# Attention and two MLPs on one core: the first product of each MLP by seven Strassen products, its result kept in DRAM, the second product summed in PSUM

## The chip, the cores and the metric

One core of a Trainium2 chip runs the whole program. The metric is device time in microseconds; three runs of the kernel before lie between 1133.15 and 1134.03 us. The engines are named as in the profile: PE (matmuls) with PEld (its weight loads), DVE (VectorE), ACT (ScalarE), POOL (GpSimd), SP (the DMA queue that issues nearly all transfers).

## The reference

Sigmoid attention over 4 batches, 12 heads, 448 tokens and 64 columns per head, then two MLPs on the 1792 x 768 result, each 768 -> 2048 -> 768. All weights arrive as 64-bit floats; everything else is 32-bit.

```python
scores = scale * np.matmul(q, k.transpose(0, 1, 3, 2)) - np.log(S)
attn = 1.0 / (1.0 + np.exp(-scores))
x = np.matmul(attn, v)                       # then (B*S, H*D) = (1792, 768)
h = x @ w_in                                 # layer 0, w_in 768 x 2048
g = np.where(h > 0.0, h, np.exp(np.minimum(h, 0.0)) - 1.0)
x = g @ w_out
h = x @ w_in                                 # layer 1
g = h - np.tanh(h)
out = g @ w_out
```

## The kernel before, in words

Each operand of a matmul is split into a head (rounded to the matmul's type) and a rest, and every product of 128x128 weights is three matmuls: head by head, head by rest, rest by head. A split is one ACT copy (head) and one DVE subtraction (rest).

**Order.** `Sched` takes operations with a queue, an estimated cost, what they come after and a rank, simulates the five queues and emits in the order that this gives. On a chip each engine runs its queue in that order. Attention's operations are chained per queue by the due times of `PHASES`; those of the MLP come in by their rank.

**Attention.** 24 pairs of heads. Per pair: transposes of q and k, scores (L344), sigmoid (L355), its split `ah` (L364 to L370), `pv` (L382) into one PSUM tile, the values' split on POOL (L329, L334). `xhead` (ACT, L389) and `xrest` (DVE, L394) put the result, split, into X; the next pair's first `pv` waits for `xrest`.

**MLP.** Per layer 8 groups of two hidden chunks of 128 (`GC`, `NG`). For each group and each of four token blocks (512, 384, 384, 512 wide: `AT`) `m_h` (L547) makes each chunk's 18 matmuls: 6 slices of the 768 inputs, three matmuls each. `g_a`, `g_b`, `g_c` (L553 to L573) apply the nonlinearity, `g_head` and `g_rest` (L580, L584) split it, `m_o` (L588 to L615) makes the group's share of the second product, and `p_add` (L617 to L623) adds it to the sum P in SBUF; the first group is a copy by ACT (L621). So first and second products alternate. At layer 0's end `x_head` and `x_rest` (L626, L629) split P into X; at layer 1's end `store` writes P to `out`.

**Weights.** Each chunk of 128x768 64-bit values is loaded (L486) into one of two buffers, `first` and `second`, narrowed to 32 bits by one ACT and three DVE operations (L496 to L511) and split (L524, L528). The load of a chunk waits for the split of the chunk two before it.

## Time and profile before

| | |
|---|---|
| runs, median (range) | 1133.44 us (1133.15 to 1134.03), 3 runs |
| profiled execution, first to last instruction | 1131.9 us, 1.5 us under the median |
| PE / PEld busy | 1122.2 / 1025.5 us |
| DVE / ACT / POOL busy | 727.7 / 476.4 / 61.6 us |
| granted PE clock | 1.00 throughout |
| attention's last `pv` ends | 204.9 us |
| DMA moved | 73.3 MB, mean 65 GB/s |

The chain of waits goes back from the last instruction to what released it, so its shares say what the time was spent on in a row; a group row has an operation's busy time, the mean of one in ns, and the idle time of its engine just before. Durations reported for neighbouring operations overlap by some 0.07 us on DVE.

### The profile page before, as it was taken

To read this page: it belongs to the slowest core of one execution; us is meant where nothing else is said; L and a number is where in the kernel's file an instruction comes from. 1 tells how busy PE (TensorE), PEld (TensorE's weight loads), DVE (VectorE), ACT (ScalarE), POOL (GpSimd) and SP (SyncE) were. 2 spreads that over 40 slices of the span, in tenths; PEclk is the share of its full clock that TensorE was granted. 3 is DMA by queue.
4 is the path that set the end of the run, shared out by engine and by line. 5 is a ranking of instruction groups with operands and counts; after the bars stand their busy time and mean duration, and the time that the engine had idled before them with its cause. 6 is when DMAs were issued, how large, how long until landed. Compare 5 with 4: busy or idle time off the path is not lost.

```text
span 1131.9 us, 14882 instructions
## 1 busy us (share of the span) xinstructions
PE 1122.2 (99%) x6020; PEld 1025.5 (91%) x6020; DVE 727.7 (64%) x1117; ACT 476.4 (42%) x743; POOL 61.6 (5%) x112
## 2 busy tenths in 40 slices
PE   8999999999999999999999999999999999999998
PEld 7888888998989898989898989999999999999897
DVE  6888889735575757575757793557474847575644
ACT  6777778654333333333334554523131313131310
POOL 4323223000000000000000000000000000000000
PEclk9999999999999999999999999999999999999999
DMA  6334332211111111111202020303020202121124
GB/s 157 89 82 98 84 81 84 85 56 56 56 56 56 56 56 57 54 58 38 75 29 84 28 84 22 91 4 96 14 86 27 84 28 84 29 84 28 56 66 130
DMA packets 86900, 73.31 MB, mean 65 GB/s; under 512 B 50096, under 2 KB 81072, under 8 KB 86832
## 3 DMA queue, kind: packets, MB, share of 16 engines
q1 hardware_dynamic: 85312, 71.85, 21.8%
q8 instruction: 47, 0.77, 0.3%
q10 hardware_dynamic: 1520, 0.52, 0.2%
q14 instruction: 21, 0.17, 0.0%
HBM read 66.85 MB, written 5.51 MB: 64 GB/s over the span
## 4 chain that ended last, share of the span: by engine, by line
PE 98%; SPq 0%; DMA 0%; POOL 0%; DVE 0%; ACT 0%; issue 0%; ACTq 0%
PE hps L547 41%; PE ops L610 21%; PE ops L597 20%; PE pvps L382 9%; PE sps L344 5%; PE tps L302 2%; DMA first<-in_q_dram 0%; SPq L233 0%; ACT a L355 0%; DVE ah L370 0%; POOL vs L329 0%; SPq L214 0%; POOL vs L334 0%; DVE ah L366 0%; SPq L237 0%
## 5 line engine op out<-in xcount | busy, mean ns | idle before, releaser
L623 DVE TENSOR_TENSOR P<-P,ops 128x384 f32<-128x384 f32 (+1 forms) x364 | 209.4, 580 | 62.0 <-PE ops L610 33.9
L547 PE MATMUL hps<-X,e 128*128 128x512 f32 (+1 forms) x1152 | 242.2, 363 | 0.0
L547 PE MATMUL hps<-X,wi 128*128 128x512 f32 (+1 forms) x1152 | 240.7, 362 | 0.0
L610 PE MATMUL ops<-wo,g 128*128 128x384 f32 x1344 | 238.3, 334 | 0.0
L597 PE MATMUL ops<-g,wo 128*128 128x512 f32 (+1 forms) x1152 | 235.8, 362 | 0.0
L610 PEld LDWEIGHTS ops<-wo,g 128*128 128x128 f32 x1344 | 234.0, 188 | 1.2
L597 PEld LDWEIGHTS ops<-g,wo 128*128 128x128 f32 x1152 | 208.4, 188 | 22.8
L547 PEld LDWEIGHTS hps<-X,e 128*128 128x128 f32 x1152 | 208.6, 188 | 22.5
L547 PEld LDWEIGHTS hps<-X,wi 128*128 128x128 f32 x1152 | 208.4, 188 | 22.7 <-DVE r L571 0.2
L382 PE MATMUL pvps<-ah,vs 128*128 128x448 f32 x504 | 122.8, 377 | 1.1 <-POOL vs L334 1.1
L580 ACT ACTIVATE g<-r 128x512 fp32r<-128x512 f32 (+1 forms) x128 | 73.9, 577 | 83.5 <-DVE r L573 48.0
L584 DVE TENSOR_TENSOR g<-r,g 128x512 fp32r<-128x512 f32 (+1 forms) x128 | 79.7, 622 | 44.9 <-ACT g L580 43.8
L382 PEld LDWEIGHTS pvps<-ah,vs 128*128 128x128 f32 x504 | 89.7, 188 | 13.7 <-issue 6.8
L560 ACT ACTIVATE r<-hps 128x512 f32<-128x512 f32 (+1 forms) x64 | 34.7, 542 | 144.8 <-PE hps L547 144.8
L370 DVE TENSOR_TENSOR ah<-a,ah 128x896 fp32r<-128x896 f32 x96 | 92.9, 988 | 3.2
L573 DVE TENSOR_TENSOR r<-hps,r 128x512 f32<-128x512 f32 (+1 forms) x64 | 39.8, 621 | 83.9 <-ACT r L560 83.8
L355 ACT ACTIVATE a<-sps,bias 128x896 f32<-128x896 f32 x96 | 85.1, 916 | 3.6 <-DVE ah L370 2.5
L571 DVE SCALAR_TENSOR_TENSOR r<-r,hps 128x512 f32<-128x512 f32 (+1 forms) x64 | 39.5, 617 | 66.8 <-ACT r L564 65.0
L558 ACT ACTIVATE r<-hps 128x512 f32<-128x512 f32 (+1 forms) x64 | 34.6, 541 | 109.8 <-PE hps L547 109.6
L344 PE MATMUL sps<-e 64*128 64x448 f32 (+1 forms) x504 | 69.2, 373 | 0.4 <-ACT a L355 0.4
L528 DVE TENSOR_TENSOR e<-first,e 128x768 fp32r<-128x768 f32 x16 | 15.3, 957 | 77.8 <-ACT e L524 77.8
L344 PEld LDWEIGHTS sps<-e 64*128 64x128 f32 (+1 forms) x504 | 52.7, 185 | 11.0 <-issue 6.3
(61 smaller groups left out, 685.4 us busy)
## 6 DMA issues: line engine op xcount, KB each, us to landing
first<-in_moe_w_in_dram SPq DMA_DIRECT2D x16, 768.0 KB, 4.7
second<-in_moe_w_in_dram SPq DMA_DIRECT2D x16, 768.0 KB, 4.6
first<-in_moe_w_out_dram SPq DMA_DIRECT2D x16, 768.0 KB, 4.4
second<-in_moe_w_out_dram SPq DMA_DIRECT2D x16, 768.0 KB, 4.2
kq<-in_q_dram SPq DMA_DIRECT2D x24, 112.0 KB, 2.7
first<-in_q_dram SPq DMA_DIRECT2D x22, 112.0 KB, 2.4
kq<-in_k_dram SPq DMA_DIRECT2D x18, 128.0 KB, 2.6
vl<-in_v_dram SPq DMA_DIRECT2D x12, 192.0 KB, 2.7
```

The source lines that it names most:

```text
L344: nc.tensor.matmul(out=ps[:, j, :S], lhsT=e[lanes, ks, cols], rhs=e[lanes, qs, :S], start=(x == 0), stop=(x == 2),)
L355: nc.scalar.activation(out=a[:, :m], in_=T.pop(("s", n, u))[:, :m, :S], func=ACTF.Sigmoid, bias=bias, scale=scale)
L370: nc.vector.tensor_tensor(out=t[:, 1, :m], in0=T.pop(("a", n, u))[:, :m], in1=f(t[:, 0, :m]), op=ALU.subtract)
L382: nc.tensor.matmul(out=ps, lhsT=vs[n % 2][:, vz, c:c + 128], rhs=t[:, az, j], start=(u == 0 and j == 0 and vz == 0 and az == 0), stop=(u = ...
L547: nc.tensor.matmul(out=ps, lhsT=wi[wz][:, kk], rhs=X[:, xz, kk, tokens(b)], start=(n == 0), stop=(n == 3 * KD - 1),)
L571: nc.vector.scalar_tensor_tensor(out=r, in0=r, scalar=-1.0, in1=h, op0=ALU.add, op1=ALU.max)
L573: nc.vector.tensor_tensor(out=r, in0=h, in1=r, op=ALU.subtract)
L580: nc.scalar.activation(out=gt[:, 0, c, half(b)], in_=T["g", i, g, b, c], func=ACTF.Copy)
L584: nc.vector.tensor_tensor(out=gt[:, 1, c, half(b)], in0=T.pop(("g", i, g, b, c)), in1=f(gt[:, 0, c, half(b)]), op=ALU.subtract)
L597: nc.tensor.matmul(out=ps, lhsT=wo[c][wz][:, e], rhs=gt[:, gz, c, half(b)], start=(n == 0), stop=(n == last),)
L610: nc.tensor.matmul(out=ps, lhsT=gt[:, gz, c, t0:t0 + 128], rhs=wo[c][wz].rearrange("p k f -> p (k f)")[:, e * DH:(e + 1) * DH], start=(n = ...
L623: nc.vector.tensor_tensor(out=acc, in0=acc, in1=ps, op=ALU.add)
```

## The change

Attention writes its result unsplit (`xdone` instead of `xhead` and `xrest`) into four tiles R0a, R0b, R1a, R1b: token half (1024 and 768 tokens) by half of the 768 columns. The MLP of a layer is two phases.

**Phase 1** has 8 groups of two hidden chunks by two token halves, called steps. With the two chunks, the two halves of the 768 inputs and the two halves of a step's tokens (512 or 384 each) as a 2x2 by 2x2 block product, `m_p` makes seven products of 9 matmuls (3 slices, three matmuls each) where eight would do it directly. Seven operands of each token half (B11, B21, B22 and the sums T1 to T4) are made once per layer; the weight side's sums S1 to S4 are made per group by POOL. Products that share a term share a PSUM bank: the bank is copied out (`snap`, ACT) and then summed onto by the next product, and `h_add` (DVE) joins it with the third. The nonlinearity follows, and `g_store` writes the hidden values unsplit to DRAM.

**Phase 2** goes over token blocks (512, 512, 384, 384 in layer 0; four of 384 and one of 256 in layer 1). For each of the 16 chunks it loads the hidden values back, splits them, and sums all 16 in PSUM over 48 matmuls per output tile; one copy takes the tile out. All of `w_out` lies split in SBUF, in the places of phase 1's operands. Twelve (layer 0) and 13 (layer 1) chunks of `w_out`, the 16 of layer 1's `w_in` and 2 of layer 0's are narrowed ahead and kept in DRAM as 32-bit values (`keep`); four chunks are narrowed during attention.

PE's order after attention is one written chain; in it each step's P4 stands behind the next step's P1. Other MLP operations are ranked by how late they may start. Core of the diff:

```diff
-            def xhead(n):
+            def xdone(n):
                 b, hp = pairs[n]
...
+                ps = T.pop(("o", n))
+                for z in range(2):
+                    lo, hi = max(b * S, T0[z]), min((b + 1) * S, T0[z] + 2 * HW[z])
+                    if lo < hi:
+                        t = raws[f"R{z}" + "ab"[hp // KH], 0].rearrange("p (k t) -> p k t", k=KH)
+                        nc.scalar.activation(
+                            out=t[:, hp % KH, lo - T0[z]:hi - T0[z]], in_=ps[:, lo - b * S:hi - b * S], func=ACTF.Copy
+                        )
...
+                if place == "W2":
+                    return ("R0a", 3 * CW, 4 * CW), ("R0b", 3 * CW, 4 * CW)
...
+            def w_sum(step, which, j0, j1):
...
+                out, x, y, op = {
+                    "S1": (s1, a21, a22, ALU.add), "S2": (s2, s1, a11, ALU.subtract),
+                    "S4": (s4, a12, s2, ALU.subtract), "S3": (s3, a11, a21, ALU.subtract),
+                }[which]
+                nc.gpsimd.tensor_tensor(out=out, in0=x, in1=y, op=op)
...
+            SUMS = {"T1": ("12", "12", "11"), "T2": ("12", "22", "12"), "T3": ("11", "12", "11"), "T4": ("21", "21", "12")}
...
+            def sums_on(i, s, x):
+                return "POOL" if (i, s) == (0, 1) and x != "T1" else "DVE"
...
+            PROD = {
+                "P1": ("B11", "W0", 0, "a", True), "P2": ("B21", "W0", 1, "b", True),
+                "P5": ("T1", "W1", 0, "d", True), "P6": ("T2", "W1", 1, "a", False),
+                "P3": ("B22", "W2", 1, "d", False), "P7": ("T3", "W2", 0, "a", False),
+                "P4": ("T4", "W3", 0, "a", False),
+            }
...
+            def m_p(step, p):
...
                 n = 0
-                for kk in range(KD):
+                for kk in range(KH):
                     for wz, xz in ((0, 0), (0, 1), (1, 0)):
+                        k0 = (half * KH + kk) * 128
                         nc.tensor.matmul(
-                            out=ps, lhsT=wi[wz][:, kk], rhs=X[:, xz, kk, tokens(b)],
-                            start=(n == 0), stop=(n == 3 * KD - 1),
+                            out=ps, lhsT=w[wz][:, k0:k0 + 128], rhs=xs[xz][:, kk],
+                            start=(opens and n == 0), stop=(n == 3 * KH - 1), skip_group_check=True,
                         )
                         n += 1
...
+            SNAP = {"s1": "a", "s2": "a", "s5": "d"}
+            ADD = {(0, 0): ("s1", "b"), (0, 1): ("s2", "d"), (1, 1): ("s5", "a")}
+
+            def snap(step, x):
+                s = step[2]
+                T["s", step, x] = t = temp(slot_of["s", step, x])[:, :HW[s]]
+                nc.scalar.activation(out=t, in_=T["ps", step, SNAP[x]], func=ACTF.Copy)
+
+            def h_add(step, c, b):
+                x, tag = ADD[c, b]
+                t = T["s", step, x]
+                nc.vector.tensor_tensor(out=t, in0=t, in1=T["ps", step, tag], op=ALU.add)
...
+                nc.sync.dma_start(
+                    out=hidden[i, n][:, t0:t0 + HW[s]], in_=T.pop(("s", step, "o" if (c, b) == (1, 0) else ADD[c, b][0]))
+                )
...
+            def g_load(i, k, n):
+                t0, w = blocks(i)[k]
+                T["graw", i, k, n] = t = temp(slot_of["graw", i, k, n])[:, :w]
+                nc.sync.dma_start(out=t, in_=hidden[i, n][:, t0:t0 + w])
...
+            PRODS = ("P1", "P2", "P5", "P6", "P3", "P7")
...
+                    ps = [("h", step, p) for p in PRODS]
+                    if n:
+                        ps.insert(1, ("h", mine_steps[n - 1], "P4"))
+                    sequence += ps
...
+                after = {
+                    "P6": [("snap", step, "s1")], "P3": [("snap", step, "s5")],
+                    "P7": [("snap", step, "s2")], "P4": [("h_add", step, 1, 1)],
+                }
...
+            sch.chain([("pv", last, 3)] + sequence)
```

## Rows read from the trace of the kernel before

**Rows 1.** The page, part 1: busy us of each engine (share of the span).

```profile
PE 1122.2 (99%) x6020; PEld 1025.5 (91%) x6020; DVE 727.7 (64%) x1117; ACT 476.4 (42%) x743; POOL 61.6 (5%) x112
```

**Rows 2.** The page, part 4: the chain that ended last, by engine, by line.

```profile
PE 98%; SPq 0%; DMA 0%; POOL 0%; DVE 0%; ACT 0%; issue 0%; ACTq 0%
PE hps L547 41%; PE ops L610 21%; PE ops L597 20%; PE pvps L382 9%; PE sps L344 5%; PE tps L302 2%; DMA first<-in_q_dram 0%; SPq L233 0%; ACT a L355 0%; DVE ah L370 0%; POOL vs L329 0%; SPq L214 0%; POOL vs L334 0%; DVE ah L366 0%; SPq L237 0%
```

**Rows 3.** Windows: busy us of each engine (instructions), PEclk, DMA share, GB/s.

```profile
0.00:15.00 15.00, 10.71 (x73) 9.05 (x73) 5.25 (x8) 6.84 (x10) 10.21 (x24) 1.00 0.72 168
...
250.00:650.00 400.00, 400.00 (x1992) 359.83 (x1991) 250.54 (x389) 150.74 (x241) 0.00 (x0) 1.00 0.17 54
```

**Rows 4.** The chain in order of time: start, us, what (one piece of each width).

```profile
236.24 8.20 PE hps L547 x36
...
267.06 6.26 PE hps L547 x36
```

**Rows 5.** Groups by line: busy us, mean ns of one, idle before.

```profile
L623 DVE TENSOR_TENSOR P<-P,ops 128x384 f32<-128x384 f32 (+1 forms) x364 | 209.4, 580 | 62.0 <-PE ops L610 33.9 <-PE ops L597 25.6
...
L571 DVE SCALAR_TENSOR_TENSOR r<-r,hps 128x512 f32<-128x512 f32 (+1 forms) x64 | 39.5, 617 | 66.8 <-ACT r L564 65.0 <-issue 1.8
L564 ACT ACTIVATE r<-r 128x512 f32<-128x512 f32 (+1 forms) x64 | 37.1, 579 | 1.9
L499 DVE TENSOR_SCALAR first<-first 128x768 int32<-128x768 int32 x64 | 35.5, 555 | 4.5 <-ACT first L496 4.3
...
L558 ACT ACTIVATE r<-hps 128x512 f32<-128x512 f32 (+1 forms) x64 | 34.6, 541 | 109.8 <-PE hps L547 109.6
...
L509 DVE SCALAR_TENSOR_TENSOR first<-first 128x768 int32<-128x768 int32 x32 | 30.8, 962 | 0.6
...
L504 DVE SCALAR_TENSOR_TENSOR first<-first 128x768 int32<-128x768 int32 x32 | 30.5, 954 | 0.4
...
L496 ACT ACTIVATE first<-second 128x768 f32<-128x768 f32 x32 | 29.1, 911 | 47.6 <-DVE first L504 47.6
...
L528 DVE TENSOR_TENSOR wi<-second,wi 128x768 fp32r<-128x768 f32 x16 | 15.3, 957 | 18.6 <-ACT wi L524 18.6
```

**Rows 6.** Timeline at the end of attention: start, us, engine, line, operation.

```profile
196.37 4.27 PE L547 MATMUL hps<-X,e 128*128 128x512 f32 x18
...
196.90 0.54 ACT L389 ACTIVATE X<-pvps 128x448 fp32r<-128x448 f32 x1
...
198.58 0.61 DVE L394 TENSOR_TENSOR X<-pvps,X 128x448 fp32r<-128x448 f32 x1
199.11 1.61 DVE L370 TENSOR_TENSOR ah<-a,ah 128x896 fp32r<-128x896 f32 x2
...
200.47 4.42 PE L382 MATMUL pvps<-ah,vs 128*128 128x448 f32 x21
...
200.72 0.60 ACT L558 ACTIVATE r<-hps 128x512 f32<-128x512 f32 x1
```

**Rows 7.** Timeline of POOL, DVE and PE in attention's last 30 us.

```profile
173.44 1.45 POOL L334 TENSOR_TENSOR vs<-second,vs 128x256 fp32r<-128x256 f32 x2
...
174.75 1.63 DVE L370 TENSOR_TENSOR ah<-a,ah 128x896 fp32r<-128x896 f32 x2
...
182.17 2.28 POOL L334 TENSOR_TENSOR vs<-vl,vs 128x256 fp32r<-128x256 f32 x2
...
182.71 2.23 DVE L370 TENSOR_TENSOR ah<-a,ah 128x896 fp32r<-128x896 f32 x2
...
189.91 2.98 POOL L334 TENSOR_TENSOR vs<-vl,vs 128x256 fp32r<-128x256 f32 x2
...
191.43 2.67 PE L382 MATMUL pvps<-ah,vs 128*128 128x448 f32 x12 [1.06 <-POOL vs L334]
```

**Rows 8.** Line L334 by itself: duration ns min/median/max, first and last start.

```profile
L334 POOL TENSOR_TENSOR vs<-vl,vs x24: 736/744/1589, 22.7 to 191.3; 128x256 fp32r<-128x256 f32 x24
```

**Rows 9.** The page, part 6: DMA issues, KB each, us to landing.

```profile
first<-in_moe_w_in_dram SPq DMA_DIRECT2D x16, 768.0 KB, 4.7
```

More of the change, by code (lines that the diff above doesn't have):

```diff
@@ L120 @@
     KD = DM // 128
-    AT = (0, 512, 896, 1280, 1792)
+    KH = KD // 2
     WARM = 20
@@ new lines, in load, with narrow @@
+            def load(job, key, narrowed):
+                t = stage(job)
+                if narrowed:
+                    nc.sync.dma_start(out=t[:, :CW], in_=kept[key])
+                elif wide:
+                    nc.sync.dma_start(out=t.bitcast(I32).rearrange("p (k f) -> p k f", k=KD), in_=source(key))
+                else:
+                    nc.sync.dma_start(out=t[:, :CW].rearrange("p (k f) -> p k f", k=KD), in_=source(key))
+            def narrow(job, step):
+                t, d = stage(job), scratch(job)
+                low, high = (t.bitcast(I32).rearrange("p (f z) -> p f z", z=2)[:, :, z] for z in range(2))
@@ L544, in m_h @@
+            def m_p(step, p):
+                i, g, s = step
+                x, place, half, tag, opens = PROD[p]
+                if opens:
+                    T["ps", step, tag] = bank(h_bank(step, tag))[:, :HW[s]]
+                ps = T["ps", step, tag]
+                w, xs = ([what(z) for z in range(2)] for what in
+                         (lambda z: at_place(place, z, i), lambda z: xo(i, s, x, z)))
                 n = 0
-                for kk in range(KD):
+                for kk in range(KH):
@@ L642, in store @@
                     (nc.scalar if e == 1 and i0 == t * 128 else nc.sync).dma_start(
[L643 removed]
+                        out=out[row:row + R * (n - 1) + 1:R, cols], in_=out_rows(t)[i0 - t * 128:i0 - t * 128 + n, cols]
                     )
                     i0 += n
[L647 to L649 removed]
@@ new lines, in mlp, with take_place, tag_take @@
+            FIRST = {"e0": [("s", NPR - 2, u) for u in range(4)], "W1": before_early, "W3": before_early,
+                     "XA": [], "XB": before_late, "R0a": [], "R0b": [], "R1a": [], "R1b": []}
+            def take_place(place, then):
+                return [d for name, lo, hi in spans(place) for d in take(name, lo, hi, then, FIRST[name])]
+            turn_of = {}
+            def tag_take(tag, then, first=()):
+                was = turn_of.get(tag, list(first))
+                turn_of[tag] = list(then)
+                return was
@@ new lines, in mlp, with job @@
+            kept_by, ready = {}, {}
+            def job(key, keeps, place, after=(), only=False, i=0):
+                n = count[0]
+                count[0] += 1
+                stage_of[n] = (place, 2 * i + 1)
+                if only and wide:
+                    in_scratch.add(n)
+                live = key not in kept_by
+                after = list(after) + list(stage_frees[place])
+                if not live:
+                    after.append(("keep", kept_by[key], key))
+                raw_op(("load", n), "SP", 600, lambda: load(n, key, not live), after, 5400 if live else 3900)
+                done = ("load", n)
+                if place == 4:
+                    fixed[done] = 3 * CYCLE + n
+                free = scratch_free[(0, 0, 1, 2, 2)[place]]
+                if live and wide:
+                    for step, (queue, cost) in enumerate((("ACT", 910), ("DVE", 570), ("DVE", 960), ("DVE", 1050))):
+                        raw_op(("narrow", n, step), queue, cost, lambda step=step: narrow(n, step),
+                               [done] + (free if step == 0 else []), 100)
+                        done = ("narrow", n, step)
+                        if place == 4:
+                            fixed[done] = (4 + 2 * n) * CYCLE
+                    free[:] = [done]
+                stage_frees[place] = [done]
+                if keeps:
+                    kept_by[key] = n
+                    raw_op(("keep", n, key), "SP", 600, lambda: keep(n, key), [done], 5600)
+                    if n in in_scratch:
+                        free[:] = [("keep", n, key)]
+                    else:
+                        stage_frees[place].append(("keep", n, key))
+                return n, done
@@ new lines, in split @@
+            def split(name, i, place, from_, part, after, then):
+                n, done = from_
+                width = CW // 2 if part == "last" else CW
+                key = (i, place, n, part)
+                op("w_head", key, "ACT", act(width), w_head, [done] + after + take_place(place, then))
+                op("w_rest", key, "DVE", dve(width), w_rest, [("w_head",) + key])
+                stage_frees[3 if n in OPENING else stage_of[n][0]].append(("w_rest",) + key)
+                if n in OPENING and part == "sums":
+                    stage_frees[1].append(("w_rest",) + key)
+                ready[name] = ("w_rest",) + key
```

708 lines of the change are left out of this document (480 added, 228 removed).

## The prediction

> **What bounds the kernel now.** I read the busy shares first. TensorE is at work for 1122.2 of 1131.9 us [rows 1]. Busy alone does not show a bound, so the chain of waits comes next: 98% of it is PE, 41% of the span the first products (`hps`, L547), 21% and 20% the second products (`ops`, L610 and L597) [rows 2]. Two stretches confirm it [rows 3]: between 250 and 650 us PE is busy 400.00 of 400 us, VectorE 250.54, ScalarE 150.74, at the full granted clock; the start-up, 0 to 15 us, is where most of PE's idle time lies (10.71 busy of 15). So in the MLP a microsecond of matmul taken away is a microsecond gained, and one of any other engine is worth nothing until it makes PE wait.
>
> **What the change removes on PE.** A first-product block of 18 matmuls becomes, for two hidden chunks and two token widths, seven products of 9. Per layer that was 1152 matmuls; now it is 8 groups x 2 steps x 7 x 9 = 1008, again half 512 and half 384 wide. In the chain 36 matmuls of L547 take 8.20 us at 512 columns and 6.26 at 384 [rows 4], so 0.228 and 0.174 each. Saved per layer: 72 x 0.228 + 72 x 0.174 = 28.9 us; both layers 57.9; an eighth of the 41%, 58.0, says the same. The second products keep count and widths by their loops (1152 and 1344 matmuls): nothing. The smaller blocks bring no narrower matmul, so I charge nothing for shape.
>
> **Edits off PE's path.** The running sum `p_add` goes: 209.4 us of VectorE [rows 5]. That is worth nothing itself, PE did not wait for it, but it pays for what comes: three `snap`s on ScalarE and three `h_add`s on VectorE per step, 3.5 splits of `w_in` per group instead of 2, a split of 7 operands per token half instead of the columns of X, and four sums per group on GpSimd. In layer 0's first phase a group takes PE 63 x (0.228 + 0.174) = 25.3 us. VectorE per group: 3 `h_add` and 4 `g_c` in each of 2 steps at 0.617 (mean of the widths), 8.6; weight splits 3.5 x 0.957 = 3.3; narrowing of 2 + 12/7 = 3.7 chunks at 0.555 + 0.954 + 0.962 = 2.47, 9.2; total 21.1. ScalarE: 2 x (3 snaps and 4 `g_a` at 0.541, 4 `g_b` at 0.579), 3.5 splits and 3.7 narrowings at 0.911: 18.8 [rows 5]. Both fit, VectorE at 84%; layer 1 lacks the 2 chunks of `w_in` (narrowed under the second phase of layer 0) and stands at 16.
>
> **The new waits.** PE's order is now one written list, so a late operand stops everything behind it. P3 adds onto the bank that `s5` was copied from, with only P6 (9 matmuls, 2.05 or 1.57 us) between; P7 waits so for `s2` behind P3; P4 for an `h_add` behind the next P1. ScalarE starts about 0.25 us after PE has gone on (200.47 to 200.72), and that 512-column read of PSUM takes 0.60 [rows 6]; the chain is 0.85 us. That hides unless a 0.91 us op stands in front on that queue, and then it loses up to 0.2 us. Two or three such places in each of 32 steps: at least 0, at most, with two ops in front of each, about 0.9 a step (29 us). I take 0.25 a step in layer 0 (4 us), where both queues are full, and 0.1 in layer 1 (1.6), near the lower end because before this PE never waited in the MLP with the same engines feeding it.
>
> **GpSimd beside VectorE.** In attention one undisturbed pair of `vs` subtractions takes GpSimd 1.45 us and the pair of `ah` on VectorE 1.63; where they meet at 182 us they take 2.28 and 2.23, and at 189.9 the GpSimd pair takes 2.98 [rows 7]. VectorE lost 0.6 us, GpSimd 0.8 and 1.5, as if they took turns. GpSimd had no work in the MLP; now it has 4 sums of 384 columns a group: 0.744 median for 256 [rows 8] gives an estimated 1.1 each, 4.4 a group. Lower bound 0 (VectorE has 25.3 - 21.1 = 4.2 free), upper bound all 4.4 x 16 = 70 us; it is part of my 0.25 a step. The Trainium skill (SBUF — State Buffer, "Who interferes with whom") says why: an op of VectorE with two SBUF inputs and a GpSimd op that reads SBUF exclude each other for a whole instruction. By that rule the narrowing, the weight splits and three of four `g_c` would all be held up, and the rival below gets its weight; the trace's 0.6 us agrees.
>
> **The end of attention.** Before, 18 matmuls of L547 (4.27 us) ran at 196.37, while the last `pv`s waited for VectorE [rows 6]. Those now stand behind all of attention. The last pair's first `pv` gains, as it waits only for the ScalarE copy of the bank (done 197.44) and no longer for the subtraction (199.19); but `ah` still ends at 200.72 and work is there for 21 matmuls, 4.42 us [rows 6]. The last three can only follow 200.72, so attention ends some 201.5 to 202.5 instead of 204.9 less 4.27: 1 to 2 us lost, I take 1.2. Inside attention 15 us of `xrest` leave VectorE and some 4 narrowings (9.9), 4 sums and 3 operand rests of 1536 columns (two 768s, about 1.7 each) come: even in sum, but in bigger pieces. The row at 191.43, where PE waited 1.06 us for GpSimd after such a meeting [rows 7], is the price of one collision: 0 to 6 us, I take 2.
>
> **The opening of layer 0** is the dearest place. T2, B22, T3 and T4 of the first token half lie in memory that attention holds until its last copy, and W2 in the place of R0a and R0b, which are free only when T4 is split. From the last `pv`: copy 0.8, head 1.5, then four rests of 1.7 and W2's of 0.96 on VectorE: about 10.3 us. PE has P1, P2, P5, P6, 8.2 us, so P3 waits at least 2.1. Then seven operands of the second half (1152 columns, about 1.35 each), the P4 and P7 of both steps and GpSimd's three sums (about 3.3 each) compete. If these 10 us shut VectorE out, I walk to P7 of the second half at 33 us against 24 of pure work: 9 us. Between 2.1 and 9 I take 5, the middle, as no row shows sums of that size.
>
> **Other seams.** First to second phase, twice: places for `wo` and the first hidden chunks come free during the last step (11 us), and 12 or 13 chunks are narrowed ahead. Layer 0 to 1: VectorE must make seven operands with four sums in about 22 us, 7 x 1.35 + 4 x 1.35 = 15, beside a step's 4. 0 to 3 each; I take 1 each, 3 in all.
>
> **DRAM.** Before: 54 GB/s at 0.17 of the DMA engines, so 318 at full; start-up's small pieces 168 at 0.72, 233 at full [rows 3]. A group of layer 0's first phase now moves 3.7 loads of 768 KB (4.7 us each to landing [rows 9]), 1.7 kept copies and 8 stores of 448 columns on average: 5.4 MB, 17 us at the first rate, 23 at the second, under 25.3. A hidden chunk's store and reload lie a phase apart. I charge nothing; if the cover goes, it is the next group's weights that come late: staging is free 3.6 us into a group, load 4.7, narrowing 5.9, sums 4.4, splits 1.9, so 20.5 of the 30.9 us until P5 needs them. 10 us are spare.
>
> **Sum.** 1131.9 - 57.9 + 2 + 1.2 + 5 + 4 + 1.6 + 3 = 1090.8 of span. The median of the runs shown is 1.5 above the profiled span, which I keep: **1092 us**, own range 1083 to 1101.
>
> **Rivals.**
> - All waits hide but the two forced ones (1.2 and 2.1): 1133.4 - 57.9 + 3.3 = 1079. For it: slack of 0.6 us or more at each wait, and no wait of PE in the MLP before. Against: VectorE at 84%. Chance 0.19.
> - VectorE becomes the bound of layer 0's first phase: 21.1 plus the 4.4 of GpSimd is already 25.5 against 25.3; with a tenth of waiting for inputs, 28 a group, 2.7 x 8 = 22 in place of my 4, and the opening at 9: about 1114. For it: the meetings in [rows 7]. Against: VectorE's reported times overlap by some 0.07 each, so 21.1 is nearer 19.7. Chance 0.22.
> - Slower: GpSimd's sums hold VectorE and all of their time reaches PE, as VectorE's queue is in order and snaps, `h_add`s and splits wait behind it. 1092 - 5.6 + 70 = 1156. It decides from 47 of the 70 us on, when the gain of 41 (before this term, 47) is used up. For it: both queues in one list without knowledge of such meetings. Against: layer 1 has VectorE free for 9 us a group. Chance 0.06.
> - The gain is not there: the new order breaks up PE's pace, 7/8 of the matmuls at 8/7 of the time: 1133. Only widths seen before occur: 0.02.
>
> The forecast keeps 0.51. Two runs of this kernel can be told apart at about 0.2%, 2.3 us. Faster 0.51 + 0.19 + 0.22 = 0.92, within 0.2% 0.02, slower 0.06. The range takes the lower bound and the middle of the second rival: 1079 to 1115.
>
> **What would show it.** Right: 5732 matmuls (6020 - 288), the L547 successor near 405 us in the chain, `h` blocks of 9 at 2.05 and 1.57 us; PE idle near 27 us, most of it within 30 us after attention and P3 the first to wait, for a weight split. VectorE's total falls below 728 and shows pieces of double length beside GpSimd's. Wrong: PE waits of over 1 us in every step for VectorE or ScalarE, PE waiting for a DMA, or a granted clock below 1 after the opening.

## The result, and the profile after

The changed kernel takes **1101.04 us** (median of 4 runs, 1100.08 to 1102.18) against 1133.3 for the kernel before: a ratio of 0.9717, 95% interval 0.9703 to 0.973. The forecast was 1092, range 1079 to 1115. The profiled execution spans 1098.3 us, 33.6 less than before, where the sum had 41.1 less: the direction and the mechanism of the gain held, and 7.5 us of it are missing.

The page's first and fourth parts, which answer to [rows 1] and [rows 2]:

```profile
PE 1074.5 (98%) x5732; PEld 974.9 (89%) x5732; DVE 699.5 (64%) x916; ACT 549.0 (50%) x871; POOL 188.1 (17%) x179
...
PE 89%; DVE 7%; issue 2%; SPq 0%; ACT 0%; DMA 0%; ACTq 0%; DVEq 0%
```

5732 matmuls are 288 fewer. PE's share of the chain fell from 98 to 89%: DVE now has 7% of it. Where, the windows say (columns as in [rows 3]):

```profile
160.00:190.00 30.00, 27.91 (x171) 22.62 (x170) 29.97 (x30) 22.26 (x32) 22.38 (x17) 1.00 0.14 39
190.00:205.00 15.00, 12.84 (x67) 9.88 (x66) 14.93 (x17) 11.67 (x17) 6.49 (x6) 1.00 0.00 0
215.00:225.00 10.00, 8.08 (x28) 5.94 (x27) 7.85 (x8) 9.25 (x12) 4.20 (x3) 0.83 0.14 40
225.00:235.00 10.00, 7.28 (x30) 6.14 (x29) 10.00 (x6) 3.49 (x6) 10.00 (x5) 0.83 0.10 38
250.00:650.00 400.00, 400.00 (x1995) 360.33 (x1994) 270.31 (x356) 196.62 (x318) 38.23 (x29) 1.00 0.59 198
660.00:670.00 10.00, 8.05 (x37) 6.55 (x37) 10.00 (x9) 5.05 (x8) 5.49 (x3) 1.00 0.07 26
670.00:690.00 20.00, 20.00 (x95) 18.02 (x94) 16.08 (x23) 10.80 (x17) 0.62 (x1) 0.91 0.45 158
690.00:1080.00 390.00, 390.00 (x2119) 373.30 (x2118) 173.31 (x274) 137.84 (x242) 25.07 (x24) 1.00 0.46 150
```

PE is busy without a gap from 250 to 650 and from 690 to 1080 us. Behind the start-up and ahead of the last stores it has holes in three places: the end of attention, the opening of layer 0 and the opening of layer 1. VectorE is full there (29.97 of 30, 14.93 of 15, 10.00 of 10) except from 215 to 225 us, where it has 7.85 of 10 and ScalarE 9.25. The same two stretches of attention in the kernel before had PE at 30.00 and 13.94, VectorE at 26.48 and 13.23:

```profile
160.00:190.00 30.00, 30.00 (x192) 25.96 (x191) 26.48 (x36) 24.24 (x36) 9.86 (x15) 1.00 0.23 67
190.00:205.00 15.00, 13.94 (x69) 12.21 (x66) 13.23 (x18) 11.19 (x16) 2.89 (x2) 1.00 0.16 54
```

What PE waited for, longest first (total, times, longest); the names are those of the operand that came late, then of who made it:

```profile
PE psa L699 <- DVE t L716: 4.7, 2, 2.7
PE tps L304 <- DVE e L313: 3.3, 7, 0.8
PE psx L699 <- ACT t L711: 2.1, 1, 2.1
PE psd L699 <- DVE R0b L638: 1.9, 1, 1.9
```

The end of attention, which answers to [rows 6] (start, us): work for 21 `pv`s lies ready as before, P1 now follows them, and nothing of the MLP stands in front.

```profile
203.48 4.49 PE L384 MATMUL pvps<-ah,vs 128*128 128x448 f32 x21 [0.94 <-issue]
207.80 2.23 PE L699 MATMUL psa<-XA,e 128*128 128x512 f32 x9
```

Of the groups by line, the one that answers to L571 of [rows 5], and GpSimd's new sums (busy, mean ns of one):

```profile
L742 DVE SCALAR_TENSOR_TENSOR t<-spare,t 128x512 f32<-128x512 f32 (+1 forms) x39 | 32.3, 831 | 7.0 <-ACT spare L732 6.8
...
L624 POOL TENSOR_TENSOR first<-first,second 128x384 f32<-128x384 f32 x30 | 37.3, 1244 | 47.9 <-DVE R0b L638 46.8
```

The multiplication L742 takes 0.69 us at 512 columns and 0.56 at 384 where GpSimd has no work, as L571 did before; the mean of 831 ns, against 617, comes from those that run beside a GpSimd sum. A sum of 384 columns takes GpSimd 1.24 in this group's mean and 1.01 at the least, where the prediction had an estimated 1.1.

To compare kernels I cut the span at the starts of P1 (the first nine matmuls into `psa` of a group's first step), read from PE's timeline. "Opening" is from a layer's first P1 to its second group's. At the full-clock pitch pure matmul work takes 23.7 us in an opening (63 matmuls of each width, less the nine of the last P4, which stands behind the next P1), 409 in the rest of layer 0 (seven groups, that P4 and 1152 matmuls of the second product) and 412.3 in the rest of layer 1, to PE's end. Each row is one profiled execution; the last column is the median of the runs.

| us | attention ends | opening, layer 0 | rest of layer 0 | opening, layer 1 | rest, to span end | median |
|---|---|---|---|---|---|---|
| changed kernel | 207.8 | 35.5 | 409.9 | 27.6 | 417.5 | 1101.0 |
| sums on VectorE, replanned | 207.7 | 28.9 | 417.8 | 26.0 | 417.5 | 1099.9 |
| filler matmuls | 207.5 | 36.1 | 410.3 | 26.0 | 417.5 | 1099.4 |
| pieces, first half of layer 0 | 201.8 | 38.5 | 410.8 | 26.0 | 417.6 | 1096.8 |
| pieces everywhere | 201.9 | 40.6 | 416.2 | 24.5 | 417.8 | 1104.9 |
| pieces everywhere, sums on VectorE | 203.3 | 32.7 | 420.2 | 24.5 | 419.5 | 1100.7 |
| sums on VectorE, order kept | 207.5 | 33.6 | 410.2 | 27.6 | 417.6 | 1097.9 |
| pieces but for one half | 201.6 | 38.7 | 409.9 | 24.5 | 417.5 | 1094.8 |
| both of the last two edits | 201.4 | 35.9 | 410.5 | 24.5 | 419.6 | **1093.5** |
| weight sums twice | 207.6 | 36.2 | 429.7 | 27.6 | 418.0 | 1120.9 |
| stores twice | 208.4 | 36.3 | 416.6 | 27.6 | 417.6 | 1108.4 |
| P4 behind its own P7 (an opening holds one product more) | 207.5 | 40.0 | 421.2 | 28.8 | 428.7 | 1128.0 |
| eighth product | 207.4 | 34.8 | 439.1 | 28.0 | 442.7 | 1153.7 |

Layer 1's opening is 27.6 us in the changed kernel, with a granted clock of 0.94 over it, and 26.0 in run 3 and in the first variant of run 6, with a clock of 1.00, though their edits touch nothing of layer 1. So up to 1.5 us between two rows can be this, and not the edit.

Before, attention's last `pv` ended at 204.9 and PE's next product started at 204.7, with 4.1 us of first-product filler inside, so attention's own end was near 200.6. The balance is then: -57.9 of matmuls, +7.2 end of attention, +11.8 opening of layer 0, +0.9 rest of layer 0, +3.9 opening of layer 1, +1.1 behind PE's last matmul; together -33.0 of the measured -33.6.

### The profile page after: what moved, and what is told of

The parts are those of the page before. It is cut to its first block, busy times and chain, and to the rows that moved or that the text cites. A ratio compares the mean times of both kernels' runs of the same rounds, so it can differ in the third digit from the quotient of the medians.

```text
span 1098.3 us, 15568 instructions
## 1 busy us (share of the span) xinstructions
PE 1074.5 (98%) x5732; PEld 974.9 (89%) x5732; DVE 699.5 (64%) x916; ACT 549.0 (50%) x871; POOL 188.1 (17%) x179
## 4 chain that ended last, share of the span: by engine, by line
PE 89%; DVE 7%; issue 2%; SPq 0%; ACT 0%; DMA 0%; ACTq 0%; DVEq 0%
PE psa L699 11%; PE psd L699 10%; PE psx L699 9%; PE pvps L384 7%; PE psv L793 6%; PE psa L793 6%; PE psu L793 6%; PE psb L793 6%; PE psb L699 5%; PE psy L793 5%; PE psw L793 5%; PE psx L793 5%; PE psd L793 5%; PE sps L346 4%; DVE ah L372 2%
## 5 line engine op out<-in xcount | busy, mean ns | idle before, releaser
L778 DVE TENSOR_TENSOR XB<-t,XB 128x384 fp32r<-128x384 f32 (+2 forms) x79 | 44.8, 568 | 120.7 <-ACT XB L774 120.5
L774 ACT ACTIVATE XB<-t 128x384 fp32r<-128x384 f32 (+2 forms) x79 | 42.0, 533 | 152.9 <-PE psv L793 42.4
L699 PE MATMUL psa<-XB,W 128*128 128x512 f32 x192 | 55.5, 397 | 0.5 <-ACT t L711 0.5
L624 POOL TENSOR_TENSOR first<-first,second 128x384 f32<-128x384 f32 x30 | 37.3, 1244 | 47.9 <-DVE R0b L638 46.8
L699 PEld LDWEIGHTS psa<-XB,W 128*128 128x128 f32 x192 | 36.5, 191 | 8.6 <-ACT t L711 0.9
L793 PE MATMUL psb<-XB 128*128 128x384 f32 (+1 forms) x168 | 40.7, 350 | 0.0
L793 PE MATMUL psu<-XB 128*128 128x384 f32 (+1 forms) x168 | 40.7, 350 | 0.0
L793 PE MATMUL psv<-XB 128*128 128x384 f32 (+1 forms) x168 | 40.7, 350 | 0.0
L793 PE MATMUL psa<-XB 128*128 128x384 f32 (+1 forms) x168 | 40.7, 350 | 0.0
L313 DVE TENSOR_TENSOR e<-tps,e 128x448 fp32r<-128x448 f32 (+1 forms) x46 | 29.8, 648 | 16.2 <-ACT e L308 16.1
L732 ACT ACTIVATE spare<-spare 128x512 f32<-128x512 f32 (+1 forms) x64 | 36.7, 573 | 0.9
L742 DVE SCALAR_TENSOR_TENSOR t<-spare,t 128x512 f32<-128x512 f32 (+1 forms) x39 | 32.3, 831 | 7.0 <-ACT spare L732 6.8
```

Source lines behind the costliest of these rows:

```text
L313: nc.vector.tensor_tensor(out=e[:, to, :W], in0=T.pop(("t", n, w))[:, :W], in1=f(e[:, slot, :W]), op=ALU.subtract)
L624: nc.gpsimd.tensor_tensor(out=out, in0=x, in1=y, op=op)
L699: nc.tensor.matmul(out=ps, lhsT=w[wz][:, k0:k0 + 128], rhs=xs[xz][:, kk], start=(opens and n == 0), stop=(n == 3 * KH - 1), skip_group_che ...
L732: nc.scalar.activation(out=r, in_=r, func=ACTF.Exp, scale=-1.0)
L742: nc.vector.scalar_tensor_tensor(out=to, in0=r, scalar=-1.0, in1=h, op0=ALU.add, op1=ALU.max)
L774: nc.scalar.activation(out=at_place(g_place[i, k, n], 0, i)[:, :w], in_=T["graw", i, k, n], func=ACTF.Copy)
```

## The experiments

**1. An eighth product in each step**, nine matmuls into a free bank, result unused: is the steady state PE's?

```diff
+            def m_eight(*step):
+                ps = bank("u")
+                for x in range(9):
+                    nc.tensor.matmul(out=ps[:, :HW[step[2]]], lhsT=at_place("W0", 0, step[0])[:, :128],
+                        rhs=xo(step[0], step[2], "B11", 0)[:, 0], start=(x == 0), stop=(x == 8))
+            for step in steps:
+                sequence.insert(sequence.index(("h", step, "P2")) + 1, ("eight",) + step)
```

> Adds an eighth product of 9 matmuls to each step, into a free bank, its result unused: the changed kernel with the matmul count of the direct product. If PE alone bounds the steps, 57.9 us are added less what falls into PE's waits in the two openings: 1150 to 1159. If the steps are bound by the engines that feed PE, most of it hides: 1125 to 1145.

One run: 1153.72 us, span 1152.0, which is 53.7 over the changed kernel's, and 20 slower than the kernel before, with the same number of first-product matmuls. By stretches: the rest of layer 1 grew by 25.2 (seven groups of added products are 25.3), the rest of layer 0 by 29.2 (25.3 and new waits: PE has 2.8 idle between 250 and 650 us), the two openings by -0.7 and +0.4 although each got 3.6 of matmuls. PE alone bounds the steps; in the openings an added product is free, since PE waits there anyway. So the 57.9 of the sum is real, and its loss lies at the seams.

**2. P4 directly behind its own P7** instead of behind the next step's P1: what does the cover buy?

```diff
-                    ps = [("h", step, p) for p in PRODS]
-                    if n:
-                        ps.insert(1, ("h", mine_steps[n - 1], "P4"))
-                    sequence += ps
+                    sequence += [("h", step, p) for p in PRODS + ("P4",)]
```

> P4 stands right behind P7 of its own step instead of behind the next step's P1; nothing else. Theory (the copies and additions between products cost nothing because another product covers them): without cover each of 32 steps waits for ScalarE-free chain P7, h_add, P4 of about 0.25 + 0.6 + 0.1 us, so 1101 becomes 1125 to 1140, a wait of about 1 us of PE for VectorE in every step. Rival (VectorE is so far ahead or behind that the place of P4 does not matter): within 5 us of 1101.

One run: 1128.0 us, 27 more, 0.84 a step. The new waits are P4's, for the `h_add` that joins its bank; of the 16.3 us below, two waits with 4.7 us are in the changed kernel too:

```profile
PE psa L699 <- DVE t L716: 16.3, 13, 5.0
PE psx L699 <- DVE t L716: 7.1, 11, 0.6
```

Outside the openings nearly all of these waits are 0.65 or 0.78 us long, near the 0.85 of the prediction's chain. So that chain is there, and one neighbouring product of 1.6 to 2.1 us hides it.

**3. Operand sums on VectorE, replanned.** GpSimd's three sums of layer 0's second half go to VectorE, and the planner knows it.

```diff
-                return "POOL" if (i, s) == (0, 1) and x != "T1" else "DVE"
+                return "DVE"
```

> The three sums of layer 0's second token half (T2, T3, T4, 1152 columns) run on VectorE instead of GpSimd; nothing else. Theory (GpSimd's sums hold VectorE): in the changed kernel seven VectorE operations between 223 and 237 us took 8 us more than their like elsewhere, each beside a GpSimd sum; they go back to 0.68 and 1.35 us, three sums of 1.35 are added, the P4 wait of 2.7 us and its half-clock product (1.6) go: 1101 becomes 1095 to 1098. Rival (the opening is bound by the amount of work that stands in VectorE's queue, wherever the sums run): 4 us more on VectorE, 1101 to 1105, with P4 waiting as before.

1099.90 us (1099.72 to 1102.91), ratio 0.9712, interval 0.9698 to 0.9727: not told apart from the changed kernel, and between the times that the two theories gave. The opening lost 6.6 us, and the rest of layer 0 gave 7.9 back. The first return is seen in the timeline of ACT, PE and the store queue:

```profile
247.98 0.33 SPq L755 DMA_DIRECT2D hidden<-t  x1
...
250.40 0.60 ACT L711 ACTIVATE t<-psa 128x512 f32<-128x512 f32 x1 [3.69 <-DMA hidden<-t]
...
251.05 0.73 PE L699 MATMUL psa<-XB,R0a 128*128 128x512 f32 x2 [2.25 <-ACT t L711]
```

A `snap` needs the buffer of a hidden value whose store was issued 2.4 us earlier, and PE waits for the `snap`. Was it the work moved to VectorE, or the new order? The next run keeps the order.

**4. The same sums on VectorE, order kept**: the planner still thinks them GpSimd's.

```diff
-                by = nc.gpsimd if sums_on(i, s, x) == "POOL" else nc.vector
+                by = nc.vector
```

> Only the engine that executes the three operand sums of layer 0's second token half changes (VectorE in place of GpSimd); the planner still thinks them GpSimd's, so every other instruction keeps the order it has in the changed kernel. Theory A (the meetings of GpSimd and VectorE lengthen layer 0's opening, and the 8 us that the earlier variant with these sums on VectorE lost later came from its changed order): opening of layer 0 from 35.5 to 29 to 31 us, rest of layer 0 stays near 410, total 1094 to 1096. Theory B (what was lost later comes from the sums' work on VectorE itself, whatever the order): rest of layer 0 near 418, total 1099 to 1102.

1097.87 us (1097.37 to 1098.23), ratio 0.9689, interval 0.9673 to 0.9705. The rest of layer 0 stays at 410.2, so the 8 us of run 3 came from its order, as theory A had it. But the opening is 33.6, not 29 to 31, and the total not 1094 to 1096: with three sums of 1.35 us more in VectorE's own queue, taking them off GpSimd is worth 1.9 us there, and the other 4.7 of run 3 came with its order. VectorE's four multiplications (L742) of the step go from 3.12, 1.49, 1.50 and 0.68 us to 1.51, 1.50, 0.68 and 0.67, the weight sums remaining on GpSimd, but P7 of the second half still waits, 2.61 us (before 2.14):

```profile
236.51 1.16 ACT L668 ACTIVATE R1a<-R1b 128x1152 fp32r<-128x1152 f32 x1 [1.61 <-DVE R0b L671]
237.58 0.47 ACT L711 ACTIVATE t<-psx 128x384 f32<-128x384 f32 x1
...
238.10 1.01 PE L699 MATMUL psx<-R0b,R0a 128*128 128x384 f32 x2 [2.61 <-ACT t L711]
```

The `snap` (0.47) that releases P7 stands on ACT's queue behind the head of the last operand (1.16), which waits 1.61 for a place that VectorE has to free. In run 3 the `snap` stood in front, and PE waited 0.16. P7 starts 33.85 us after the first P1 in the changed kernel, 30.57 here and 27.27 in run 3. From there to the next P1 it is 1.67, 3.04 and 1.68: behind the wait of 2.61 the granted clock is 0.75 (235 to 241 us), which takes back 1.4 of the 3.3 us that P7 had gained.

**5. Filler matmuls** ahead of P3 and P4 in layer 0's opening (10 and 14) and ahead of P4 in layer 1's (9): does the granted clock, 0.83 in the opening, cost anything?

```diff
+            FILL = {("h", (0, 0, 0), "P3"): 10, ("h", (0, 0, 0), "P4"): 14, ("h", (1, 0, 0), "P4"): 9}
...
+            def m_fill(k, step, p):
+                ps = bank("u")
+                for _ in range(FILL["h", step, p]):
+                    nc.tensor.matmul(out=ps, lhsT=at_place("W0", 0, step[0])[:, :128],
+                        rhs=xo(step[0], 0, "B11", 0)[:, 0], start=True, stop=True)
```

> Idle matmuls into a free PSUM bank stand in front of the three products that waited 2 to 3 us: 10 before P3 and 14 before P4 of the first step, 9 before P4 of layer 1's first step; their results are not used. Theory (the wait itself lets the granted clock fall to the lower level, and the products behind it run at half pace): the clock stays at the upper level, P3 and P4 take 2.05 us from their first matmul to their last instead of up to 3.65, and 1101 becomes 1096 to 1098. Rival (the slow products are slow for their operands, or the filling costs as much as it saves): 1100 to 1103, or slower by the filling that outlasts the waits, at most 3 us.

1099.35 us (1099.30 to 1099.39), interval 0.9687 to 0.9716, overlapping the changed kernel's. P3 and P4 ran at full pace, and the opening was no shorter (36.1 against 35.5). PE waited later instead, and the lower clock came there (0.84 from 235 to 244 us):

```profile
234.84 1.66 PE L699 MATMUL psx<-XB,W 128*128 128x384 f32 x8 [1.51 <-DVE XB L671]
240.85 0.77 PE L699 MATMUL psx<-R0b,R0a 128*128 128x384 f32 x2 [2.79 <-ACT t L711]
```

P7 of the second half starts only 0.5 sooner (33.32 us after P1), because what it waits for comes no sooner, and then takes 1.1 longer at the lower pace. This run therefore moved the slow products and did not remove them. Run 1 tells more: there the granted clock stayed at 1.00 through the whole opening, with PE idle for 5.8 us, and the opening took 34.8. So the operations of VectorE, ScalarE and GpSimd bound layer 0's opening; the clock is worth little there, some 0.7 us by this comparison, in which the planner's order differs too. Layer 1's opening was 1.5 shorter, as in run 3, which has no filler; that the filler did it is not shown.

**6. Operand preparation in pieces**: a sum, head or rest of 1536 or 1152 columns as three of 512 or 384. Four variants: only the first half of layer 0; everywhere; everywhere with run 3's sums; all but the second half of layer 0.

```diff
             def pieces(i, s):
-                return (slice(None),)
+                return (0, 1, 2) if (i, s) == (0, 0) else (slice(None),)
```

> The seven operands of the first token half of layer 0 are summed and split in three pieces of 512 columns each instead of one of 1536. Theory (attention lost about 7 us of PE's time because single VectorE operations of 1.75 to 1.95 us stand in front of the split of the next transposes): no VectorE operation is longer than about 1.1 us there, attention ends 2 to 4 us earlier than 207.8, 1101 becomes 1097 to 1099. Rival (it is the amount of work on a VectorE that is 97% busy there, not its grain): same work plus 14 more starts, attention ends at 207 to 209, 1101 to 1103.

> All operand sums and splits of both layers and both token halves go in three pieces (512 or 384 columns); the second half's sums of layer 0 stay on GpSimd. Theory (long single operations make both the attention loss and part of the openings: an operation that is late holds the queue for its whole length, and a GpSimd sum of 384 columns shuts VectorE out for about 0.9 us instead of 2.7 to 3.7): attention as in the three-piece run (ends near 202), layer 0's opening shorter than that run's 38.5 us, layer 1's P4 wait of 2 us smaller; 1096.8 becomes 1088 to 1094. Rival (the openings are bound by the amount of work on VectorE and GpSimd): 1096 to 1099.

> As the run with all operands in three pieces, and layer 0's second-half sums on VectorE too, so that GpSimd is idle in the opening but for the weight sums. Theory (GpSimd's sums shut VectorE out): a further 2 to 5 us, 1086 to 1091, unless the changed order of the queues again brings waits later on, as it did with the sums alone on VectorE (4 us between 250 and 340 us, on copies that waited for a store to DRAM to free their buffer). Rival (with small pieces the two engines take turns at no loss): no better than that run, or up to 3 us slower.

> Operand preparation in three pieces for layer 0's first half and both halves of layer 1, sums where the changed kernel has them. If the 4 us that pieces everywhere lost came from cutting layer 0's second half (more meetings with GpSimd): 1093 to 1096, layer 1's opening 24.5 us, rest of layer 0 near 410. If cutting layer 1's halves costs as much in the end of layer 0: 1099 to 1105.

Only the first half: 1096.79 us (ratio 0.9679, interval 0.9663 to 0.9695). Attention ends 6.0 earlier, the opening takes 3.0 more. The planner made a new order here as well: in the changed kernel the last operand sum that runs under attention starts at 188.89 us, here those of T3 and T4 start from 201.24 on, at its end. Everywhere: 1104.92 (0.9756, interval 0.974 to 0.9772), as the rest of layer 0 loses 6.3; with the replanned sums 1100.71 (0.9715). The first of these is slower than either of its expectations allowed; the sums on VectorE give 4.2 of it back, as their theory had it. All but layer 0's second half: 1094.84 (0.9664, interval 0.9649 to 0.9678), its rest of layer 0 back at 409.9 and layer 1's opening at 24.5, 0.8 above pure work. So the 6 us come with the pieces of layer 0's second half. With pieces everywhere PE waits for 4.2 us in the rest of layer 0, and 4.0 of it stands at 310 to 427 us, for `h_add`s, a weight split and a hidden value's split, when the pieces have long been made (the last ends at 244.7). That speaks for the planner's changed order, as in run 3, but no run kept the order here.

**7. Runs 4 and 6 together**: sums on VectorE in the kept order, pieces for all but layer 0's second half.

> The variant with the sums on VectorE in the kept order, plus operand preparation in three pieces for all halves but layer 0's second. If the gains add: attention's end -6, opening -5 less the 3 that the pieces cost it, layer 1's opening -2 to -3: 1086 to 1090. If the opening is bound by VectorE's total of work whichever way it is cut: 1094 to 1097, as with the pieces of one half alone.

**1093.47 us** (1090.95 to 1094.91), ratio 0.965, interval 0.9635 to 0.9664, the fastest median here, about 7.6 under the changed kernel; against the pieces alone the intervals overlap. The gains did not add to 1086 to 1090. Attention's end did as hoped (201.4); the opening took 35.9, 2.8 less than with the pieces alone, where 33.5 was hoped for; and layer 1's rest took 2.1 more. Of these, 1.5 are two waits of PE (0.36 and 1.16 at 682.7 and 689.8); the first stands behind a `snap` that waited 1.96 us for a store of a hidden value, where without run 4's edit the same `snap` waited 0.53. Why that store landed later was not settled.

**8. GpSimd's weight sums twice** in groups 1 to 7 of both layers: how near is the slower rival?

```diff
-                nc.gpsimd.tensor_tensor(out=out, in0=x, in1=y, op=op)
+                for _ in range(2 if step[1] else 1):
+                    nc.gpsimd.tensor_tensor(out=out, in0=x, in1=y, op=op)
```

> GpSimd makes each weight sum of groups 1 to 7 twice (same result), so 4 more operations of 1.2 us in each of 14 groups, 67 us of GpSimd in all, with no change to any other queue. Theory (VectorE has 13% free in layer 0's first phase and a third in layer 1's, and this covers what GpSimd holds up): 1101 becomes 1101 to 1108, with VectorE at 95% or more in layer 0. Slower rival of the prediction (what GpSimd holds up reaches PE in full): 1150 to 1170.

One run: 1120.91 us, 19.9 more, all of it in the rest of layer 0 (+19.8), and between the two expectations. The window of the steady stretch, and one of the waits that now come once a group (274.8, 302.7, 332.4, 360.4, 388.4, 417.9 us); its line numbers are one higher:

```profile
250.00:650.00 400.00, 386.02 (x1885) 343.28 (x1884) 269.96 (x351) 191.71 (x317) 72.11 (x54) 0.99 0.60 198
...
302.73 0.62 PE L700 MATMUL psx<-R1a,e 128*128 128x384 f32 x2 [2.24 <-DVE t L717]
```

33.9 us more of GpSimd in this stretch leave PE 14.0 idle, and the granted clock falls to 0.99: with both, 58% of GpSimd's time arrives at the end. All six waits are for an `h_add` of VectorE and none for a split of the weights that the sums make, so it is not late weights that PE waits for. In layer 1, where VectorE has room (104.38 of 160 us busy between 700 and 860 in the changed kernel), 28 us more behind the opening cost 0.4.

**9. Each store of a hidden value twice**, the second to memory that nothing reads.

```diff
+                if n not in again:
+                    again[n] = store_p.tile([128, 2 * B * S], F32, name=f"again{n}", tag=f"again{n}")
+                nc.sync.dma_start(out=again[n][:, i * B * S + t0:i * B * S + t0 + HW[s]], in_=t)
```

> Each hidden piece is stored to DRAM twice, the second time to a tile that nobody reads: 29 MB more written, in layer 0's first phase about 246 GB/s become 320. Theory (the five buffers of the copies are nearly all in use; a copy waits for the store of the step before, and that has 1 to 2 us to spare): the store frees its buffer 0.5 to 2 us later, PE waits for ScalarE's copies in many steps, 1101 becomes 1106 to 1130. Rival (the transfers are hidden with room): 1100 to 1103.

One run: 1108.4 us, 7.4 more, 6.7 of it in the rest of layer 0, where PE has 3.5 idle in the steady window at 232 GB/s, by waits for `snap`s. Whether the rate does it or buffers that come free only after two stores was not told apart.

```profile
250.00:650.00 400.00, 396.52 (x1960) 354.30 (x1959) 265.87 (x358) 195.81 (x321) 33.09 (x29) 1.00 0.68 232
```

## Why the prediction was right, and where its terms were off

**PE's 57.9 us: right.** The pieces of the chain that answer to [rows 4] are products of nine matmuls, 2.04 us at 512 columns (2.08 for P1) and 1.56 or 1.58 at 384, one behind the other without a gap (start, us, what):

```profile
255.35 2.04 PE psa L699 x9
257.39 1.58 PE psx L699 x9
```

Run 1 shows the same from the other side.

**Engines beside PE: right, with less room than it looks.** VectorE was put at 84% of a group of layer 0's first phase, ScalarE at 74; the window shows 52.39 and 41.35 of 60, 87 and 69%:

```profile
300.00:360.00 60.00, 60.00 (x296) 53.43 (x295) 52.39 (x72) 41.35 (x70) 11.01 (x8) 1.00 0.71 246
```

**"0.25 a step in layer 0 (4 us), 0.1 in layer 1 (1.6)", and 2 for the seams between phases: charged too much.** Measured together: 0.9, and the second phase follows the first without a gap. P4's cover holds (run 2), and 0.85 us behind P6 or P3 is shorter than the 1.6 to 2.1 of the product between. The bound of 29 was not idle, though: run 2 lost 27 by taking one cover away.

**GpSimd beside VectorE: the mechanism right; it reaches PE in the opening and not in the steps.** In the steps of layer 0 one multiplication of 384 columns in each group takes 1.37 us instead of 0.56, and two of the four weight sums beside it 1.75 and 1.61 instead of 1.02; PE waits for none of it. In the opening's timeline (start, us):

```profile
224.40 3.75 POOL L662 TENSOR_TENSOR R1a<-R1a 128x1152 f32<-128x1152 f32 x1
225.57 3.12 DVE L742 SCALAR_TENSOR_TENSOR t<-spare,t 128x512 f32<-128x512 f32 x1
228.11 3.10 POOL L662 TENSOR_TENSOR R1b<-R1b,R1a 128x1152 f32<-128x1152 f32 x1
228.62 0.68 DVE L716 TENSOR_TENSOR t<-t,psa 128x512 f32<-128x512 f32 x1
229.22 3.21 DVE L671 TENSOR_TENSOR R0a<-R1b,R0a 128x1152 fp32r<-128x1152 f32 x1
229.35 0.86 PE L699 MATMUL psa<-XB,e 128*128 128x512 f32 x2 [2.72 <-DVE t L716]
```

A multiplication that takes 0.69 us where no GpSimd sum runs (run 3) takes 3.12 and ends 0.54 after GpSimd's sum; the `h_add` that P4 waits for, with one input in PSUM, keeps its 0.68 but stands behind it. That is what the Trainium skill (SBUF — State Buffer, "Who interferes with whom") says of an operation with two SBUF inputs and of one with a single such input outside VectorE's two-port modes, and the trace agrees on both. Run 4 gives a net price: with the three big sums on VectorE, 4 us of work there, the opening is 1.9 us shorter. What the meetings alone cost, without that work, no run shows.

**"The end of attention": 3.2 charged, 7.2 measured.** The step that failed is "even in sum, but in bigger pieces ... I take 2". It was not even: by the prediction's own figures 15 us leave VectorE and 9.9 + 7 x 1.7 = 21.8 come. Measured from 133 to 201 us, VectorE is busy for 66.97 of 68 us against 59.83 before, GpSimd for 44.16 against 21.34, and PE has 63.43 against 66.94. The windows of the kernel before, the changed kernel and the first variant of run 6, in this order; the last two lines are the changed kernel and the variant again:

```profile
133.00:201.00 68.00, 66.94 (x411) 57.51 (x410) 59.83 (x81) 53.92 (x78) 21.34 (x32) 1.00 0.32 83
133.00:201.00 68.00, 63.43 (x384) 51.37 (x383) 66.97 (x70) 52.47 (x77) 44.16 (x36) 1.00 0.22 54
133.00:201.00 68.00, 65.93 (x405) 56.40 (x404) 65.11 (x78) 55.35 (x86) 35.13 (x36) 1.00 0.22 54
133.00:160.00 27.00, 25.74 (x164) 21.42 (x164) 26.04 (x29) 22.54 (x36) 15.29 (x15) 1.00 0.39 92
133.00:160.00 27.00, 27.00 (x175) 23.17 (x174) 25.55 (x33) 24.24 (x41) 13.60 (x16) 1.00 0.46 110
```

Here the pair of attention that ends at 186.4 us (start, us; L396 is the copy that closes a pair):

```profile
176.29 1.97 DVE L662 TENSOR_TENSOR R0b<-R0b,R0a 128x1536 f32<-128x1536 f32 x1
...
179.39 0.61 DVE L313 TENSOR_TENSOR e<-tps,e 128x448 fp32r<-128x448 f32 x1
180.05 0.66 PE L304 MATMUL tps<-ident,kq 128*128 128x128 f32 x4 [0.19 <-DVE e L313]
...
181.69 2.62 POOL L624 TENSOR_TENSOR second<-spare 128x384 f32<-128x384 f32 x2
182.01 1.44 DVE L368 CAST ah<-a 128x896 fp32r<-128x896 f32 x1
...
185.91 0.54 ACT L396 ACTIVATE R1a<-pvps 128x448 f32<-128x448 f32 x1
```

Before, pairs followed 7.9 us apart; from 133 to 203 us they now lie 7.2 to 9.7 apart, each sum or rest of 1.35 to 1.97 us standing in VectorE's queue before the operations (L313) that free the bank of PE's next transposes, and the first weight sums beside a cast of 0.61 that takes 1.44. What the length of an operation does shows from 133 to 160 us: VectorE is nearly as busy in the variant with pieces (25.55 against 26.04), and there PE has no gap, against 1.26 us. But the 6.0 us by which run 6 ends attention earlier are not length alone. That variant also makes the sums of T3, T4 and the second half's T1 behind attention, some 5 us of VectorE's work, and its opening is 3.0 longer. So more work on a VectorE that was full, and longer operations in its queue, made the 7.2 together; no run keeps them apart.

**"The opening of layer 0": 5 charged, 11.8 measured, above the upper bound of 9.** P3 was the first long wait, 1.92 us for a weight split, as foretold (2.1 at least; the terms given for it add up to 10.1 and not 10.3, which makes it 1.9). The walk "to P7 of the second half at 33 us" was good: P7 starts 33.85 after P1. But if the 33 is P7's start, "against 24 of pure work" sets it against the time of its end; to its start pure work is 22.1, so the bound should have read 11. And I took the middle where the walk had given a time. The runs divide the 11.8 in part: the three big sums on VectorE instead of GpSimd give back 1.9 (run 4), a different order of ScalarE's and VectorE's queues with them another 4.7 (run 3 against run 4), and the clock some 0.7 (run 1), which may be part of the others. At least 4 us were not divided further, with VectorE at 10.00 of 10 us from 225 to 235.

**"Other seams ... I take 1 each": 3.9 for layer 0 to 1.** Here too the sums and rests of 1.35 to 2.17 us stand in front of the `h_add` that P4 waits for (1.95 us), and the granted clock of 0.91 behind it costs 1.5. In pieces P4 waits 0.46 instead, the clock stays at 1.00, and the opening is 24.5: 0.8 over pure work, the size that I had charged.

**DRAM: nothing charged, and nothing seen** in the changed kernel, at 198 GB/s over the steady stretch. Of the page's transfers, those that answer to [rows 9] and the new ones (KB each, us from issue to landing):

```profile
hidden<-t SPq DMA_DIRECT2D x52, 256.0 KB, 2.0
first<-in_moe_w_in_dram SPq DMA_DIRECT2D x14, 768.0 KB, 5.1
...
t<-hidden SPq DMA_DIRECT2D x53, 192.0 KB, 2.4
hidden<-t SPq DMA_DIRECT2D x51, 192.0 KB, 3.4
```

A load of weights takes 5.1 us instead of 4.7, and the 10 us that were spare swallow that. Run 9 shows that the margin is small: with every store twice, 17% more traffic in the steady stretch, 7.4 us are lost, by the rate or by buffers that come free later.

**The end of the program** had no term and costs 1.1 (5.1 us from PE's last matmul to the end, 4.0 before): the last four output tiles end 0.52 us apart, and five of their stores stand in one queue (2.21 us from the first issue to the last).

```profile
1092.76 0.49 ACT L811 ACTIVATE R1b<-psu 128x384 f32<-128x384 f32 x1 [0.55 <-PE psu L793]
1092.87 2.21 SPq L827 DMA_DIRECT2D out_dram<-R1b  x5
1093.29 0.56 DVE L813 COPY R1b<-psv 128x384 f32<-128x384 f32 x1 [0.49 <-PE psv L793]
```

**The rivals.** "All waits hide" fell by the seams. "VectorE the bound of layer 0's first phase", 1114, took its opening right (9 and more) and its steps wrong (0.9 in place of 22). The slower rival's mechanism exists: by run 8, 58% of GpSimd's added time reaches the end in layer 0's steps, where VectorE has 13% free, and next to none in layer 1's. The sums that the kernel has cost nothing in the steps; how much more GpSimd work it would take before PE waits, between once and twice the sums, was not tried.

**The signs.** 5732 matmuls, VectorE below 728 us and P3's wait came as named. PE idles 23.8 us where 27 were named, but only 5.1 of it within 30 us after attention and not most: 5.5 lie in attention behind the start-up. One sign of being wrong came too: the granted clock is below 1 behind layer 0's opening, 0.91 in layer 1's.

**How near 1092 was.** The terms for the steps and for the seams between the phases were some 7 us too high, those for the end of attention, the two openings and the end of the program some 15 too low. That the sum missed by 8 and not by 15 is luck.

## What to carry to other kernels

A matmul less is worth its whole time where PE shows no gap, and an added one there costs all of it, so look for the loss first at the seams, where operands of a new form must be made before the first product can run. Walk such a seam to one named instruction, in one unit on both sides, and take the walk, not the middle between it and nothing. Count what a full engine loses and gains in one sum before calling it even. Long operations on a queue that also feeds PE cost by their length besides: in pieces, with VectorE as busy, a stretch of 27 us lost its 1.26 us of waits. But where three engines are full, a replanned order took 6 to 8 us elsewhere, so test a change of engine or size with the order kept.

## What the runs showed of the hardware that was not expected

- A cast with one SBUF input, 0.61 us alone, took 1.44 and 1.43 beside GpSimd's sums: the meeting is not limited to operations with two inputs. The Trainium skill (SBUF — State Buffer, "Who interferes with whom") names casts in VectorE's two-port modes among those that can meet GpSimd; the trace agrees that a cast does, and does not show its mode.
- Layer 1's P4 waited 1.94 to 1.95 us in the changed kernel, in run 3 and in run 4. In the first and the last the granted clock then fell (0.90 in 672 to 680 and 0.79 in 664 to 672), with openings of 27.6; in run 3 it stayed at 1.00 and the opening was 26.0. From P1 to the end of P4's wait PE did the same in all three, to within 0.05 us.
- A store of 192 or 256 KB lands 3.4 or 2.0 us after its issue (medians of the page), so a buffer that is stored and at once needed again is late by about as much: two of the waits that the variants added are of this kind.
